# Filling products on TensorE, and new costs and ranks for the planner of a fused attention and two-layer kernel

## The chip, the cores and the metric

One core of a Trainium2 chip runs the whole program. The metric is the device time of one execution in microseconds (us). The profiled execution is a single one; the time of the kernel is the median of several.

## The reference

```python
def _attn_ref(q, k, v):                       # q, k, v: (4, 8, 576, 64)
    scores = scale * np.matmul(q, k.transpose(0, 1, 3, 2))
    mask_plain = (rel >= 0) & (rel < 32)
    mask_dil = (rel >= 0) & (rel < 128) & (rel % 4 == 0)
    ...                                        # plain for heads 0-3, dilated for heads 4-7
    scores = np.where(masks[None], scores, -1e9)
    attn = np.exp(scores - max); attn = attn / (sum + 1e-9)
    return np.matmul(attn, v)

def reference(**kwargs):
    x = attn_out.transpose(0, 2, 1, 3).reshape(2304, 512)
    x = _moe_ref(x, w_in, w_out)      # h = x @ w_in; (h - tanh(h)) @ w_out
    return _moe2_ref(x, w_in, w_out)  # h = x @ w_in; (h * sigmoid(h)) @ w_out
```

The weights are 512 x 2048 and 2048 x 512 for each layer, and arrive as 64-bit numbers.

## The kernel before

Attention is done for a batch at a time, in four pairs of heads; pairs 0 and 1 are plain, 2 and 3 dilated. A pair has nine query blocks of 64 rows, worked in three units of three blocks. In the first batch a unit is: mask and score products into a bank y0 or y1 (`products`, L425 and L432), the maxima on VectorE (L456), the exps with their sums on ScalarE (L469), a reciprocal and the normalisation on VectorE or GpSimd (L474 to L479), the transposition of P on TensorE (L501), its copy to pT on ScalarE (L127 by `p_copy`), the product with v (`values`, L510), and a split of the result into two parts, `x_hi` on ScalarE and `x_lo` on VectorE (L529). Ahead of a pair, q and k are transposed on TensorE (L387 for dilated pairs, L396 for plain ones). In later batches VectorE transposes instead (L416, L492).

Each layer has 16 steps f. A first product `h` takes four chunks c of the 512 features with three passes each (`passes`, L541); a gate (ScalarE and VectorE) gives g, split into two parts; a second product `y` adds into four banks y0 to y3. The first block of 512 tokens needs x of all four pairs of the first batch; the second batch is worked while that block runs.

The weights come in 32 chunks per layer (16 for `w_in`, 16 for `w_out`). A chunk is loaded into a staging buffer (L144, L146), then scaled in two ScalarE passes (`prelu` L160, `lows` L165), shifted on VectorE (L170), joined on GpSimd (L174), copied as the leading part on ScalarE (L127, w) and subtracted for the trailing part (L183).

The order of everything up to the second product of step 13 of the first block is set by a planner. `play` (L93) holds a list of operations, each with the engines it may run on and a cost in us, the operations it follows, a rank, and for loads a landing time `late`. It repeatedly takes the operation that can begin first, by the planned times; of those that begin within 0.02 us on the same engine it takes the one of the lowest rank; and it emits its instructions at once. Each engine's queue is then worked in this order, whatever the true durations are. Chunk work has the rank `due`, step f of the first block `SLOT0 + SLOT * f`, units of the first batch 12 to 32, and pairs of the second batch `NEXT0 + NEXT * c`. The landing of loads is planned as one running sum over all loads. The planner starts TensorE at 6.3 us.

Before it, `WARM` products of 512 columns run on TensorE while the first loads arrive (L723 to L726). The banks y0 and y1 take the scores of units in turn, y2 and y3 the transposed P (`y_bank`, L746).

The lines which a walk through the plan needs are these.

```python
106                for e, c in o.on.items():
107                    if begins[e] + c <= soon:
109            t, e = min((min(x[0] for x in v), e) for e, v in first.items())
110            t, o = min((x for x in first[e] if x[0] <= t + NEAR), key=lambda x: x[1].rank)
117                landed = max(landed, t + 1.5) + o.late
118                o.end = landed + 0.7
```

Of the kernel before, what the change touches and what calls it, by code (L numbers as in the profile page):

```python
# [8 lines left out]
F32 = mybir.dt.float32  # L9
F32R = mybir.dt.float32r  # L10
BF16 = mybir.dt.bfloat16
# [8 lines left out]
P = 128  # L20
QB = 64
ROWS_P, ROWS_D = 96, 72
KB = 96
UB = 3
# [7 lines left out]
def tile_kernel(  # L32
# [47 lines left out]
    class Op:  # L80
# [8 lines left out]
        def shares(self, e):  # L89

            return self.port and e in "VP"

    def play(ops, free):  # L93


        landed = port = 0.0
        todo = list(ops)
        while todo:
            first = {}
            for o in todo:  # L100
                if any(a.end is None for a in o.after):
                    continue
                ready = max((a.end for a in o.after), default=0.0)
                begins = {e: max(free[e], ready, port if o.shares(e) else 0.0) for e in o.on}
                soon = min(begins[e] + c for e, c in o.on.items()) + SLACK
                for e, c in o.on.items():
                    if begins[e] + c <= soon:
                        first.setdefault(e, []).append((begins[e], o))
            t, e = min((min(x[0] for x in v), e) for e, v in first.items())
            t, o = min((x for x in first[e] if x[0] <= t + NEAR), key=lambda x: x[1].rank)  # L110
            o.fn(ENGINE[e])
            free[e] = t + o.on[e]
            if o.shares(e):
                port = free[e]
            o.end = free[e] + JOIN
            if o.late:
                landed = max(landed, t + 1.5) + o.late
                o.end = landed + 0.7
            todo.remove(o)
# [150 lines left out]
    for n in range(NB):  # L270

        for start in range(0, S, CLS):
            at = start - (QB * n - HALO)
            if 0 < at < KB:
                keep(half[:, n, 0:at], [[0, at]], at - HALO - 1, -1)
    nc.scalar.copy(out=mask[QB:], in_=half)
    mask_dil = [mask[:, UB * u:UB * (u + 1)] for u in range(NU)]
    mask_plain = [mask[:, 0::5]] + [mask[:, NB - 1:]] * (NU - 1)

# [263 lines left out]
    class First:  # L543
# [29 lines left out]
        def second_part(self, f, c, g):  # L573
            w = wout[0, f]
            if c == 0 and f == 0:
                self.y = [ps_y.tile([P, 512], F32, tag=f"y{k}", name=f"y{k}")[:, :self.n] for k in range(NC)]
            if True:
                passes(self.y[c], [w[:, a, c * P:(c + 1) * P] for a in range(2)],
                       [g[:, a] for a in range(2)], f == 0, f == NF - 1)
                if f == NF - 1:  # L580
                    hi, lo = self.parts(c)
                    nc.scalar.activation(out=hi, in_=self.y[c], func=AF.Copy)
                    nc.vector.tensor_tensor(out=lo, in0=self.y[c], in1=hi.bitcast(F32), op=ALU.subtract)
# [64 lines left out]
    ATTN_END = max(max(x) for x in STARTS) + 10  # L648


    MORE_OUT = (28, 29, 30, 31)
    MORE_IN = (14, 16, 18, 20, 22, 24, 26, 28)
    WARM = 14

    SLOT0, SLOT, UNIT0, UNIT = 46.0, 5.2, 12.0, 1.8
    DUE = 13.0
    NEXT0, NEXT = 41.0, 20.0
    SLACK, NEAR, JOIN = 0.3, 0.02, 0.05  # L660

    FEED2 = ((1, 1, 1), (1, 1, 2))
# [29 lines left out]
    with tc.manual_schedule():  # L692
# [11 lines left out]
        def op(on, fn, after=(), rank=0.0, late=0.0, port=False):  # L704
            ops.append(Op(on, fn, after, rank, late, port))
            return ops[-1]
# [29 lines left out]
        for p in first:  # L736
            got[p, 0] = op({"S": 1.1 if p.dil else 0.55}, lambda e, p=p: p.load_q(), rank=p.c, late=0.8)
            got[p, 1] = op({"S": 1.1 if p.dil else 0.55}, lambda e, p=p: p.load_k(), rank=p.c + 0.1, late=0.8)
            v_on = {"P": 0.62} if p.dil else {"S": 0.55}
            got[p, "v"] = [op(v_on, fn, rank=p.c + 0.2, late=0.25 if p.dil else 0.5) for fn in p.v_loads()]  # L740
        ring_h, ring_s, ring_t, ring_o, ring_p = (Ring(2) for _ in range(5))
        ring_v = Ring(UB)
        x_done = {}
        early = {}

        def y_bank(n):  # L746
            return ps_y.tile([P, 512], F32, tag=f"y{n}", name=f"y{n}")

        for i, (p, u) in enumerate(units):
            r = p.rank + UNIT * u  # L750
            if u == 0:
                moves = []
                for which in range(2):
                    for half in range(2):
                        held = {}
                        a = op({"T": 0.8}, lambda e, p=p, w=which, h=half, held=held: held.update(m=p.transpose_pe(w, h)),
                               [got[p, which], *ring_h.take()], r - 2 + which * 0.1)
                        moves.append(op({"V": 0.34, "A": 0.36}, lambda e, p=p, w=which, held=held: p.transposed(e, w, held["m"]),
                                        [a], r - 2 + which * 0.1))
# [2 lines left out]
                in_room[2 * p.c + 1] = moves[2:]  # L762
                free_p = ring_p.take()
                early[p] = []
            a = op({"T": 1.0}, lambda e, p=p, u=u, i=i: p.masked_scores(u, y_bank(i % 2)), [*moves, *ring_s.take(), *free_p], r)
            early[p].append(a)
            b = op({"V": 0.38}, lambda e, p=p, u=u: p.maxima(u), [a], r)
            c = op({"A": 1.35}, lambda e, p=p, u=u: p.exps(u), [b], r)
            ring_s.leave(c)
            d = op({"V": 0.36}, lambda e, p=p, u=u: p.sums(UB * u, UB * (u + 1)), [c], r)  # L770
            d = op({"V": 0.4, "P": 0.65}, lambda e, p=p, u=u: p.normed(e, UB * u, UB * (u + 1)), [d], r, port=True)
            t = op({"T": 0.45}, lambda e, p=p, u=u, i=i: p.p_transpose_pe(u, y_bank(2 + i % 2)), [d, *ring_t.take()], r)
            if u == NU - 1:
                ring_p.leave(t)
            m = op({"A": 0.4}, lambda e, p=p, u=u: p.p_copy(e, u), [t, *ring_v.take()], r)
            ring_t.leave(m)
            a = op({"T": 0.6}, lambda e, p=p, u=u, i=i: p.values(UB * u, UB * (u + 1), *((ps_s, "s") if i % 2 else (ps_o, "o"))),
                   [m, *got[p, "v"], *ring_o.take()], r)
            ring_v.leave(a)
            b = op({"A": 0.4}, lambda e, p=p, u=u: p.x_hi(e, UB * u), [a], r)  # L780
# [228 lines left out]
```

## Time and profile before

| | |
|---|---|
| median of 3 runs | 915.97 us (915.05 to 916.33) |
| the profiled execution | 915.71 us, its span 913.9 us |
| TensorE busy | 896.9 us (98%), 5998 products |
| VectorE busy | 436.0 us (48%) |
| ScalarE busy | 398.0 us (44%) |
| GpSimd busy | 122.6 us (13%) |
| mean granted TensorE clock | 0.986 |

The span is the time from the first to the last instruction of the profiled execution. PE is TensorE, DVE VectorE, ACT ScalarE, POOL GpSimd, SP the queue of SyncE. "Busy" counts the time in which an engine has at least one instruction in work; products overlap in TensorE's pipeline, so the durations of single ones add up to more. The granted clock is given as a share of 2.4 GHz. A releaser behind an arrow is the instruction that ended the idle time before.

### The profile page before, as it was taken

What the parts mean: (1) busy time and instruction counts of PE and PEld (TensorE: products, weight loads), DVE (VectorE), ACT (ScalarE), POOL (GpSimd) and SP (SyncE); (2) the same over time, 40 slices, a digit from 0 to 9 for tenths busy, and PEclk for the clock granted to TensorE, in tenths of its full rate; (3) what the DMA queues carried; (4) which work ended last, traced back from release to release, by engine and by line L of the source; (5) the groups of instructions that cost most, each with busy time, mean ns of one, the idle gap of its engine ahead of it and who ended that gap; (6) DMA issues with size and microseconds to landing.
All of it is one profiled execution on the core that took longest, in us unless ns stands there. A gap on an engine that the chain in (4) does not pass through costs nothing.

```text
span 913.9 us, 15235 instructions
## 1 busy us (share of the span) xinstructions
PE 896.9 (98%) x5998; PEld 782.8 (86%) x5998; DVE 436.0 (48%) x836; ACT 398.0 (44%) x969; POOL 122.6 (13%) x164
## 2 busy tenths in 40 slices
PE   7999999999999999999999999999999999999997
PEld 5677778999999999999999888888888888888896
DVE  2468887446756666433266666422222222222232
ACT  5689875334443334423266666432223222322322
POOL 8333553000010000000022222100000000000000
PEclk9599999999999999999999999999999999999999
DMA  9966335213223322024044564140004000200100
GB/s 232 281 153 167 98 96 117 93 28 82 49 50 58 97 35 69 20 70 147 1 141 139 186 214 139 46 136 3 1 1 139 0 1 1 93 0 1 32 15 24
DMA packets 122375, 74.39 MB, mean 81 GB/s; under 512 B 84896, under 2 KB 110528, under 8 KB 122304
## 3 DMA queue, kind: packets, MB, share of 16 engines
q1 hardware_dynamic: 121472, 72.57, 28.6%
q0 software_dynamic: 832, 0.85, 0.4%
q8 instruction: 47, 0.77, 0.4%
q14 instruction: 24, 0.20, 0.1%
HBM read 59.24 MB, written 14.16 MB: 80 GB/s over the span
## 4 chain that ended last, share of the span: by engine, by line
PE 85%; DVE 5%; ACT 4%; issue 2%; DMA 2%; SPq 2%; DVEq 0%; ACTq 0%
PE h L541 39%; PE y L541 39%; PE s L432 3%; PE o L510 2%; DMA st<-in_moe_w_in_dram 1%; ACT w L127 1%; ACT st L160 1%; DVE g L555 1%; DVE pT L492 1%; SPq L359 1%; PE y L432 1%; PE h L387 1%; ACT gg L969 1%; DVE w L183 1%; DVE st L170 1%
## 5 line engine op out<-in xcount | busy, mean ns | idle before, releaser
L541 PE MATMUL h<-x,w 128*128 128x512 f32 (+4 forms) x2304 | 439.5, 338 | 0.8
L541 PEld LDWEIGHTS h<-x,w 128*128 128x128 f32 x2304 | 365.6, 188 | 45.2 <-DVE g L555 2.5
L541 PE MATMUL y<-gg,w 128*128 128x304 f32 (+3 forms) x1344 | 226.8, 314 | 0.0
L541 PE MATMUL y<-w,gg 128*128 128x512 f32 x864 | 209.8, 390 | 0.4 <-ACT gg L969 0.4
L541 PEld LDWEIGHTS y<-gg,w 128*128 128x128 f32 x1344 | 197.6, 188 | 8.8 <-DVE gg L882 0.7
L541 PEld LDWEIGHTS y<-w,gg 128*128 128x128 f32 x864 | 160.8, 188 | 34.3 <-ACT gg L969 1.2
L969 ACT ACTIVATE gg<-g 128x512 fp32r<-128x512 f32 (+4 forms) x176 | 90.7, 515 | 134.5 <-DVE g L555 74.6
L604 DVE SCALAR_TENSOR_TENSOR g<-g,h 128x512 f32<-128x512 f32 (+1 forms) x80 | 50.7, 633 | 200.6 <-ACT g L603 200.6
L971 DVE TENSOR_TENSOR gg<-g,gg 128x512 fp32r<-128x512 f32 (+4 forms) x176 | 96.9, 550 | 102.4 <-ACT gg L969 99.3
L603 ACT ACTIVATE g<-h 128x512 f32<-128x512 f32 (+1 forms) x80 | 44.4, 555 | 201.9 <-PE h L541 201.7
L174 POOL TENSOR_TENSOR st<-st 128x512 int32<-128x512 int32 x64 | 67.3, 1053 | 211.8 <-ACT st L165 179.2
L554 ACT ACTIVATE g<-h 128x304 f32<-128x304 f32 (+2 forms) x96 | 40.2, 418 | 122.6 <-PE h L541 117.8
L555 DVE TENSOR_TENSOR g<-h,g 128x304 f32<-128x304 f32 (+2 forms) x96 | 44.6, 465 | 82.3 <-ACT g L554 81.9
L183 DVE TENSOR_TENSOR w<-st,w 128x512 fp32r<-128x512 f32 x58 | 53.9, 933 | 24.0 <-ACT w L127 23.8
L160 ACT ACTIVATE st<-st 128x512 f32<-128x512 f32 x64 | 43.0, 671 | 8.9 <-DMA st<-in_moe_w_out_dram 4.5
L492 DVE STREAM_TRANSPOSE pT<-prob 32x288 f32<-32x288 f32 x96 | 44.9, 468 | 1.5
L127 ACT ACTIVATE w<-st 128x512 fp32r<-128x512 f32 x64 | 42.4, 664 | 4.0 <-POOL st L174 3.4
L165 ACT ACTIVATE st<-st 128x512 int32<-128x512 uint32 x64 | 43.3, 677 | 0.0
L469 ACT ACTIVATE prob<-prob,nb 128x96 f32<-128x96 f32 x108 | 38.8, 364 | 0.2 <-DVE nb L456 0.2
L479 POOL TENSOR_TENSOR prob<-prob,sum 128x864 f32<-128x864 f32 (+1 forms) x17 | 20.1, 1182 | 114.7 <-DVE sum L475 114.7
L170 DVE TENSOR_SCALAR st<-st 128x512 uint32<-128x512 uint32 x64 | 28.6, 455 | 6.6 <-ACT st L160 4.9
L510 PEld LDWEIGHTS o<-pT,v 96*64 96x64 f32 x576 | 21.6, 146 | 11.8 <-issue 4.3
(61 smaller groups left out, 421.2 us busy)
## 6 DMA issues: line engine op xcount, KB each, us to landing
st<-in_moe_w_in_dram SPq DMA_DIRECT2D x64, 256.0 KB
st<-in_moe_w_out_dram SPq DMA_DIRECT2D x32, 512.0 KB
x<-y_hi SPq DMA_DIRECT2D x4, 1024.0 KB
x<-y_lo SPq DMA_DIRECT2D x4, 1024.0 KB
qin<-in_q_dram SPq DMA_DIRECT2D x48, 72.0 KB
kin<-in_k_dram SPq DMA_DIRECT2D x48, 72.0 KB
v<-in_v_dram SPq DMA_DIRECT2D x16, 192.0 KB
y_hi<-x SPq DMA_DIRECT2D x3, 608.0 KB
```

Source lines behind the costliest of these rows:

```text
L127: engine.activation(out=out, in_=in_, func=AF.Copy, scale=1.0 if scale is None else scale)
L160: engine.activation(out=high, in_=high, func=AF.Prelu, scale=2.0 ** -112, alpha=2.0 ** 32)
L165: engine.activation(out=low.bitcast(I32), in_=low, func=AF.Copy, scale=2.0 ** -29)
L174: engine.tensor_tensor(out=high, in0=high, in1=self.low.bitcast(I32), op=ALU.add)
L183: engine.tensor_tensor(out=self.flat[:, 1], in0=self.high.bitcast(F32), in1=self.flat[:, 0].bitcast(F32), op=ALU.subtract)
L492: nc.vector.transpose(out=pT[32 * kk:32 * kk + 32, :, j, 32 * i:32 * i + 32], in_=self.p[p0:p0 + 32, :, 32 * kk:32 * kk + 32],)
L541: nc.tensor.matmul(o, stat[a], mov[b], start=first and n == 0, stop=last and n == 2)
L555: nc.vector.tensor_tensor(out=g, in0=h, in1=g, op=ALU.subtract)
L603: nc.scalar.activation(out=g, in_=h, func=AF.Tanh, scale=0.5)
L604: nc.vector.scalar_tensor_tensor(out=g, in0=g, scalar=1.0, in1=h, op0=ALU.add, op1=ALU.mult)
L969: nc.scalar.activation(out=gg[:, 0], in_=g, func=AF.Copy)
L971: nc.vector.tensor_tensor(out=gg[:, 1], in0=g, in1=gg[:, 0].bitcast(F32), op=ALU.subtract)
```

## The change

Filling products: `play` gets a function `idle`. When the operation that it takes next is on TensorE, and TensorE's planned idle time before it is long enough, it first emits products of a 128 x 128 bf16 identity with 224 columns of the mask, whose results nobody reads. Their number is the idle time less `IDLE_GAP`, over `IDLE_US`, rounded down; before 12 us of planned time 0.4 us is added to the idle time. They go to columns 288 to 511 of a bank that is `lent`: first the bank of the warming products, then the bank of the scores emitted last, whose columns 0 to 287 hold these scores. With the first second product of the first block, `lent` is emptied and no more are emitted.

Costs and ranks: the planner's costs of TensorE's small products become smaller. `WARM` goes from 14 to 18. `DUE`, which is subtracted in the rank of chunk work, goes from 13 to 6; `NEXT0` and `NEXT` from 41 and 20 to 60 and 16; the first of `MORE_OUT` from 28 to 27, which is the chunk number up to which one extra staging buffer is used.

```diff
+    def idle(us):
+
+        for n in range(int((us - IDLE_GAP) / IDLE_US) if lent else 0):
+            nc.tensor.matmul(lent[0][:, UB * KB:], one[BF16], spare, start=True, stop=True)
 
     def play(ops, free):
 ...
             t, o = min((x for x in first[e] if x[0] <= t + NEAR), key=lambda x: x[1].rank)
+            if e == "T":
+                idle(t - free[e] + (MORE_IDLE if t < 12.0 else 0.0))
             o.fn(ENGINE[e])
 ...
+    spare = mask[:, 0:3].rearrange("p n k -> p (n k)")[:, :512 - UB * KB]
+    lent = []
 ...
             if c == 0 and f == 0:
+                lent.clear()
                 self.y = [ps_y.tile([P, 512], F32, tag=f"y{k}", name=f"y{k}")[:, :self.n] for k in range(NC)]
 ...
-    MORE_OUT = (28, 29, 30, 31)
+    MORE_OUT = (27, 29, 30, 31)
     MORE_IN = (14, 16, 18, 20, 22, 24, 26, 28)
-    WARM = 14
+    WARM = 18
+
+    IDLE_GAP, IDLE_US = 0.3, 0.11
+    MORE_IDLE = 0.4
 ...
-    DUE = 13.0
-    NEXT0, NEXT = 41.0, 20.0
+    DUE = 6.0
+    NEXT0, NEXT = 60.0, 16.0
 ...
+        lent[:] = [bank]
 ...
         def y_bank(n):
-            return ps_y.tile([P, 512], F32, tag=f"y{n}", name=f"y{n}")
+            bank = ps_y.tile([P, 512], F32, tag=f"y{n}", name=f"y{n}")
+            if n < 2:
+                lent[:] = [bank]
+            return bank
 ...
-                        a = op({"T": 0.8}, lambda ...: held.update(m=p.transpose_pe(w, h)),
+                        a = op({"T": 0.5 if p.dil else 0.58}, lambda ...: held.update(m=p.transpose_pe(w, h)),
 ...
-            a = op({"T": 1.0}, lambda ...: p.masked_scores(u, y_bank(i % 2)), ...)
+            a = op({"T": 0.8}, lambda ...: p.masked_scores(u, y_bank(i % 2)), ...)
 ...
-            t = op({"T": 0.45}, lambda ...: p.p_transpose_pe(u, y_bank(2 + i % 2)), ...)
+            t = op({"T": 0.35}, lambda ...: p.p_transpose_pe(u, y_bank(2 + i % 2)), ...)
 ...
-            a = op({"T": 0.6}, lambda ...: p.values(UB * u, UB * (u + 1), ...), ...)
+            a = op({"T": 0.5}, lambda ...: p.values(UB * u, UB * (u + 1), ...), ...)
```

## Rows read from the trace of the kernel before

Times are us from the span's start unless the row says ns. A row of an engine's order of time has its start, its length (overlapping the next by the pipeline), and in brackets the idle time before it; a row of the chain has a start and the time until the next step.

**Rows 1.** The profile's page: busy us and share; granted clock in 40 slices.

```profile
PE 896.9 (98%) x5998; PEld 782.8 (86%) x5998; DVE 436.0 (48%) x836; ACT 398.0 (44%) x969; POOL 122.6 (13%) x164
...
PEclk9599999999999999999999999999999999999999
```

**Rows 2.** Busy time by stretch: stretch, its length, busy of each engine, clock, DMA.

```profile
20.00:25.00 5.00, 1.11 (x30) 0.84 (x27) 2.00 (x7) 3.26 (x16) 4.07 (x7) 0.98 1.08 332
25.00:48.00 23.00, 22.36 (x237) 17.04 (x237) 10.63 (x30) 14.91 (x51) 8.18 (x11) 0.50 1.00 283
48.00:60.00 12.00, 11.06 (x125) 8.24 (x122) 8.17 (x21) 10.16 (x33) 4.85 (x8) 0.97 0.39 94
60.00:110.00 50.00, 50.00 (x349) 38.00 (x348) 43.35 (x85) 46.44 (x116) 19.42 (x21) 1.00 0.57 143
110.00:160.00 50.00, 49.82 (x308) 39.55 (x307) 40.43 (x73) 32.48 (x74) 23.47 (x24) 1.00 0.47 107
160.00:913.00 753.00, 745.84 (x4736) 668.01 (x4734) 325.19 (x605) 280.28 (x654) 46.34 (x53) 1.00 0.22 64
```

**Rows 3.** The same for TensorE by single microseconds: busy, clock, DMA.

```profile
25.00:26.00 1.00, 0.99 (x7) 0.50 1.08 305
...
48.00:49.00 1.00, 1.00 (x17) 0.66 0.16 49
```

**Rows 4.** TensorE in order of time: products with idle time before them.

```profile
24.10 0.57 PE L510 MATMUL o<-pT,v 96*64 96x64 f32 x12 [3.56 <-ACT pT L127]
...
28.29 0.88 PE L501 MATMUL y<-one,prob 128*96 128x128 f32 x3 [0.62 <-POOL prob L479]
...
58.82 0.78 PE L432 MATMUL s<-kT,qT 64*64 64x32 f32 x16 [0.94 <-DVE x L529]
```

**Rows 5.** ScalarE in order of time: the first weight scaling.

```profile
21.74 0.65 ACT L160 ACTIVATE st<-st 128x512 f32<-128x512 f32 x1 [3.75 <-DMA st<-in_moe_w_in_dram]
```

**Rows 6.** The chain that ended last, in order of time.

```profile
22.39 0.97 ACT prob L469 x6
...
31.83 0.84 PE o L510 x12
...
36.54 1.16 PE y L432 x12
37.70 0.81 PE y L501 x3
...
50.25 0.64 PE y L432 x12
50.89 0.50 PE o L510 x12
51.39 0.46 PE y L501 x3
...
64.27 0.68 PE y L541 x3
```

**Rows 7.** ScalarE's groups, 20 to 59 us: count, busy us, mean ns, idle before.

```profile
L469 ACT ACTIVATE prob<-y,nb 128x96 f32<-128x96 f32 x27 | 8.8, 334 | 1.8 <-DVE nb L456 1.8
...
L127 ACT ACTIVATE pT<-y 96x384 f32<-96x384 f32 x10 | 4.9, 488 | 4.7 <-PE y L501 4.7
L127 ACT ACTIVATE x<-o 128x192 fp32r<-128x192 f32 x11 | 4.5, 407 | 2.2 <-PE o L510 2.0
L165 ACT ACTIVATE st<-st 128x512 int32<-128x512 uint32 x6 | 4.0, 670 | 0.0
```

**Rows 8.** TensorE in order of time: the warming products.

```profile
1.47 4.57 PE L725 MATMUL y<-warm 128*128 128x512 bf16 x14 [1.47 <-DVE warm L721]
```

**Rows 9.** ScalarE in order of time: the last chunk's leading copy.

```profile
153.84 0.67 ACT L127 ACTIVATE w<-st 128x512 fp32r<-128x512 f32 x1 [0.51 <-DVE w L183]
```

**Rows 10.** GpSimd in order of time: last value loads, first normalisation.

```profile
26.29 1.25 POOL L359 DMA_DIRECT2D v<-in_v_dram  x2 [0.67 <-DMA v<-in_v_dram]
27.55 0.68 POOL L479 TENSOR_TENSOR prob<-prob,sum 128x288 f32<-128x288 f32 x1
```

More of the change, by code (lines that the diff above doesn't have):

```diff
@@ L755, in tile_kernel @@
                         held = {}
-                        a = op({"T": 0.8}, lambda e, p=p, w=which, h=half, held=held: held.update(m=p.transpose_pe(w, h)),
+                        a = op({"T": 0.5 if p.dil else 0.58}, lambda e, p=p, w=which, h=half, held=held: held.update(m=p.transpose_pe(w, h)),
                                [got[p, which], *ring_h.take()], r - 2 + which * 0.1)
@@ L764, in tile_kernel @@
                 early[p] = []
-            a = op({"T": 1.0}, lambda e, p=p, u=u, i=i: p.masked_scores(u, y_bank(i % 2)), [*moves, *ring_s.take(), *free_p], r)
+            a = op({"T": 0.8}, lambda e, p=p, u=u, i=i: p.masked_scores(u, y_bank(i % 2)), [*moves, *ring_s.take(), *free_p], r)
             early[p].append(a)
@@ L771, in tile_kernel @@
             d = op({"V": 0.4, "P": 0.65}, lambda e, p=p, u=u: p.normed(e, UB * u, UB * (u + 1)), [d], r, port=True)
-            t = op({"T": 0.45}, lambda e, p=p, u=u, i=i: p.p_transpose_pe(u, y_bank(2 + i % 2)), [d, *ring_t.take()], r)
+            t = op({"T": 0.35}, lambda e, p=p, u=u, i=i: p.p_transpose_pe(u, y_bank(2 + i % 2)), [d, *ring_t.take()], r)
             if u == NU - 1:
@@ L776, in tile_kernel @@
             ring_t.leave(m)
-            a = op({"T": 0.6}, lambda e, p=p, u=u, i=i: p.values(UB * u, UB * (u + 1), *((ps_s, "s") if i % 2 else (ps_o, "o"))),
+            a = op({"T": 0.5}, lambda e, p=p, u=u, i=i: p.values(UB * u, UB * (u + 1), *((ps_s, "s") if i % 2 else (ps_o, "o"))),
                    [m, *got[p, "v"], *ring_o.take()], r)
```

## The prediction

> **What bounds the kernel now.** I read four views in this order: the page's busy line and clock line, busy time by stretch, TensorE's instructions in order of time, and the chain that ended last. The page says that TensorE is busy for 98% of the span and that its clock is full in every slice but one [rows 1]. So the end is set by TensorE, and what a change can give back is time in which TensorE is idle or slow. The stretches say where that is: nearly all of it lies in the first 60 us [rows 2]. From 60 to 160 us TensorE is busy for 99.8 of 100 us at full clock, and from 160 us on for 745.8 of 753. The reader should see two losses in the early stretches. Between 20 and 25 us TensorE works for 1.1 of 5 us. From 25 to 48 us it is busy for 22.4 of 23 us, but the granted clock is 0.50, that is 1.2 GHz. By single microseconds the clock falls after that hole and comes back in the 49th [rows 3].
>
> The hole has a cause that can be followed. TensorE waits 3.56 us before a values group (L510) for ScalarE's copy of pT [rows 4]. ScalarE is late because its in-order queue stands 3.75 us at the first scaling of a weight chunk (L160, prelu of chunk 0), whose DMA has not landed before 21.7 us [rows 5]. The planner put that prelu ahead of the exps of the fourth and fifth unit, which follow it as the chain's six exps at 22.39 us [rows 6]; it believed in an earlier landing. So the stall is a misfit of plan and DMA, and its consequence is the long stretch at half clock.
>
> **What the losses are worth.** The chain gives the same groups at both clocks [rows 6]: scores 1.16 and 0.64 us, P transposes 0.81 and 0.46, values 0.84 and 0.50. The ratios are 0.55, 0.57 and 0.60. TensorE's 22.4 us between 25 and 48 us would be 22.4 x 0.55 to 0.60 = 12.3 to 13.4 us at full clock, so 9.0 to 10.1 us are lost to the clock. Idle time ahead of products adds 3.56 + 0.62 + 0.94 = 5.1 us [rows 4]. The ceiling is thus 10.1 + 5.1 = 15.2 us.
>
> **The change part by part.** *Costs and ranks.* Per unit of three query blocks the plan charged TensorE 1.0 + 0.45 + 0.6 and a third of four moves of 0.8, in all 3.1 us, or 37 us for 12 units; now it is 0.8 + 0.35 + 0.5 and four moves of 0.54 over three, 2.4 us or 28 us. Measured at full clock, P transposes and values are 0.46 and 0.50 and scores 0.64 without their mask product [rows 6], so the new numbers are nearer. I walked through the planner's rule by hand with the new costs. Chunk 0's planned landing doesn't move: SyncE's plan reaches it at 11.5 us, and the running landing time is then 2.0 + 8 x 0.8 for q and k + 8 x 0.5 for v + 9 x 0.25 for GpSimd's loads + 1.5 = 16.15, with 0.7 on top 16.9. The scores of the fourth and fifth unit are planned at 13.7 and 15.8 us, their exps at 16.3 and 18.4; with the copies behind them ScalarE is free at 20.6 with no attention work ready, and only there takes the prelu: behind the exps of the fifth unit instead of ahead of the fourth's. That puts two units of ScalarE work ahead of it, 2 x 0.97 us of exps [rows 6] and four copies of about 0.4 each [rows 7], 3.6 us, close to the 3.75 us for which it stood [rows 5]. I take the stall as gone; if chunk 0 lands later, up to the old 3.75 us stay.
>
> *Four more warming products.* Fourteen take 4.57 us [rows 8], 0.33 each, while later products of 512 columns run at 0.68 for three, 0.23 each [rows 6]; so four cost between 0.9 and 1.3 us. In the kernel before, such a delay would vanish under the wait for chunk 0. With that cover gone it counts; I take 0.9.
>
> *Filling products.* Each is a 128x128 bf16 product of 224 columns, so by the 0.23 us of a 512-column product about 0.10 us at full clock and 0.20 at half; the plan counts 0.11. The planner emits them only for planned idle time less 0.3 us, so in a plan that fits they cost nothing. Where TensorE is later than planned, they stand in its in-order queue ahead of real work. By hand the plan is packed on TensorE up to about 20.6 us, so next to none are emitted there; they come later, where ScalarE and the values of the last pair hold TensorE up. That is where the clock was low. They remove no work of another engine, so the new bound is ScalarE.
>
> *What is late next.* From 20 to 59 us ScalarE does 27 exps with their sums, nine units at 0.97 [rows 6], 8.7 us; 4.9 go on pT copies and 4.5 on x copies [rows 7]: 18.1 us of attention work. Starting at 21.7 us that ends at 39.8 at the earliest. Between it the plan must place three chunks or so, each three ScalarE passes of 0.67 us [rows 7]: 6 us more, 45.8. With the warming delay of 0.9 dense work begins at 46.7 instead of 58.8 us [rows 4]: 12.1 us earlier.
>
> *What is given back.* Chunk work is now due 6 instead of 13 us ahead of its slot, and the second batch's attention is ranked 19 us later for its first pair and 7 for its last. Fewer chunks are then ready when dense work starts. ScalarE is busy 46.4 of 50 us and VectorE 43.4 of 50 between 60 and 110 us [rows 2]. Two chunks' worth more on ScalarE is 2 x 2.0 = 4 us, and 46.4 + 4 exceeds 50 by 0.4; if it cannot spread beyond 110 us, where ScalarE has 17.5 us free, TensorE waits 0.4 to 4 us. I take 2. The last chunk's leading copy starts only at 153.84 us [rows 9], a few microseconds ahead of the end of this stage, so the supply has little slack at its end too. MORE_OUT moves one staging buffer by one chunk; no row shows a price. I bound it by one chunk's three ScalarE passes, 2.0 us either way [rows 7], and take 0, as only one of the last chunks is moved.
>
> *A wait that the fillers may add.* They write columns 288 to 511 of the score bank filled last, while VectorE and ScalarE read columns 0 to 287 of it. No trace here shows such a case. The price of one wait lies between 0 and one unit's exps, 0.97 us [rows 6]; over the few gaps in which those exps have started but not ended I take 1.5 us in all.
>
> The Trainium skill's page "PSUM — Partial Sum Buffer", section "PSUM bank collisions raise a hardware error", says that two engines at one bank and quadrant collide even at disjoint columns and that such accesses must be guarded by bank. By that rule every filler has to be ordered behind the reads of that bank and each later read behind the fillers; without it the 1.5 us would be 0. No run here shows it yet.
>
> **Sum.** 915.7 (the profiled run) - 12.1 + 2 + 1.5 = 907.1 us; the profiled run lies 0.3 us under the median of 915.97, within the spread of the three. I predict **907 us**, with its own range from 901 (nearly the whole ceiling, nothing given back) to 911 (four more us given back, by the bounds above).
>
> **The rivals.** *The clock falls again.* GpSimd issues the value loads of the dilated pairs until 27.55 us and only then takes a normalisation [rows 10]; TensorE already waited 0.62 us on one [rows 4]. If attention gets there earlier by the 3.75 us of the old stall, that wait grows by as much, in place of the one removed, and a hole of that size was followed by half clock before. Fillers then run at 0.20 us and delay real work, though they may also bring the clock back sooner. If half of the 12.1 us is kept, and half of the give-back of 3.5 with it, 915.7 - 6 + 1.75 = 911; 908 to 914.
> *The gain is given back later.* TensorE starts early, but chunks and second-batch attention, limited by ScalarE, VectorE and the staging loads, come at their old times, and TensorE idles between 60 and 160 us instead. For it speak 46.4 and 43.4 of 50 us; against it, that after 110 us ScalarE is only 65% busy [rows 2]. Then 914, from 912 to 916.
> *It fills nothing where it matters.* The plan sees no idle time in the 3.56 us hole, because the wait is one for a DMA that it holds landed; if the order doesn't move either, the clock falls as before: 915, 914 to 917.
> *Slower.* Every gap makes TensorE wait for the exps of the bank filled last, and the fillers run after that wait instead of during it: 0.97 + about 0.5 us of fillers per gap. What is left of the gain, 12.1 - 2 = 10.1 us, is eaten at seven such gaps, and 12 of them, one for each unit, make 12 x 1.5 = 18 us: 915.7 - 10 + 18 = 924. It decides from the eighth gap on. The page named above describes why such waits would be needed.
>
> **How the numbers follow.** Forecast 0.52, clock falls again 0.20, given back later 0.10, fills nothing 0.08, slower 0.10. A difference of 0.2%, 1.8 us, is about what a measurement of this kernel tells from none. Faster by more: 0.52 + 0.19 + 0.05 + 0.02 = 0.78. Within it: 0.01 + 0.04 + 0.05 = 0.10. Slower: 0.10 + 0.01 + 0.01 = 0.12. The range reaches from 901 to 915: it leaves out the slower case, parts of the two cases near 915, and a few in a hundred below.
>
> **What would show it.** Right: the granted clock stays at 1.00 from 20 to 60 us; ScalarE stands less than 1 us at the first L160; filling products appear after 20 us, and the second batch's first scores, now at 58.82, start near 47; TensorE is still near 50 of 50 us in the stretches behind. Wrong: a slice at 0.50 in the first 60 us (clock falls again), holes in TensorE with waits for chunks or pT between 50 and 150 us (given back), waits of the filling products for ScalarE's exps of about 1 us each (slower), or less than ten fillers (fills nothing). A first second product later than 60 us, now at 64.3 [rows 6], would refute the main term.

## The result, and the profile after

| | kernel before | kernel after |
|---|---|---|
| median (runs) | 916.15 us (915.05 to 917.30, 4) | 908.50 us (906.94 to 909.53, 4) |
| the profiled execution: time, span | 915.7 us, 913.9 us | 909.49 us, 907.7 us |
| granted clock, mean | 0.986 | 0.997 |
| instructions of TensorE | 5998 | 6028 |
| ratio, 95% interval | | 0.9915 (0.9893 to 0.9937) |

The change takes 7.7 us off, 0.85%. The prediction was 907, from 901 to 915, so the time lies inside; the steps behind it held less well than the number. Executions of one kernel differ in where the granted clock falls, so a trace shows one case, and the medians decide.

The profile's page of the kernel after, the same two lines as [rows 1]:

```profile
PE 892.7 (98%) x6028; PEld 779.9 (86%) x6028; DVE 434.3 (48%) x834; ACT 397.0 (44%) x967; POOL 130.2 (14%) x168
...
PEclk9999999999999999999999999999999999999999
```

6028 - 5998 = 30 more products: four warming ones and only 26 filling ones, all of them behind 35 us, so the 0.4 us that is added before 12 us of planned time brought none. The clock line has a 9 in every slice now.

Busy time by stretch, kernel after, columns as in [rows 2]:

```profile
20.00:25.00 5.00, 4.97 (x108) 4.01 (x106) 4.05 (x12) 3.77 (x17) 3.89 (x7) 1.00 1.09 335
25.00:48.00 23.00, 20.51 (x316) 16.29 (x313) 13.12 (x40) 16.80 (x67) 9.95 (x17) 0.93 0.95 256
110.00:160.00 50.00, 48.65 (x314) 39.39 (x313) 36.45 (x68) 31.81 (x70) 19.17 (x20) 1.00 0.41 115
```

Between 20 and 25 us TensorE works for 4.97 us instead of 1.11, and from 25 to 48 us the clock is 0.93 instead of 0.50. In that stretch it is idle for 2.5 us, 1.59 of them in one wait (below). From 110 to 160 us it is busy for 48.65 instead of 49.82: that is what is given back. Single microseconds, columns as in [rows 3], show what is left of the half clock (the clock is the first number after the five engines):

```profile
40.00:41.00 1.00, 0.12 (x2) 0.12 (x2) 0.14 (x1) 0.83 (x6) 0.24 (x1) 1.00 0.94 174
41.00:42.00 1.00, 1.00 (x10) 0.90 (x9) 0.21 (x2) 0.00 (x0) 0.61 (x1) 0.75 0.81 113
42.00:43.00 1.00, 1.00 (x7) 0.88 (x6) 0.00 (x0) 0.00 (x0) 0.06 (x1) 0.50 0.75 97
44.00:45.00 1.00, 1.00 (x8) 0.82 (x7) 0.65 (x2) 1.00 (x3) 0.00 (x0) 0.55 0.91 141
```

It falls in the 42nd and comes back in the 45th microsecond: some 3.4 us instead of the nearly 24 of [rows 3]. ScalarE in order of time, kernel after, the first weight scaling:

```profile
25.23 0.68 ACT L167 ACTIVATE st<-st 128x512 f32<-128x512 f32 x1
```

No idle time stands before it; the 3.75 us of [rows 5] are gone. It comes at 25.23 us, and the chunk had landed by 21.74 in [rows 5]. TensorE in order of time, kernel after (start, length, idle time before in brackets). L405 are transposes of q and k, L510 P transposes, L519 values, L96 filling products, L441 scores, L550 products of the chunks:

```profile
1.47 6.95 PE L738 MATMUL y<-warm 128*128 128x512 bf16 x18 [1.47 <-DVE warm L734]
...
12.14 0.72 PE L405 MATMUL h<-one,qin 96*64 96x96 f32 x12 [1.07 <-ACT kT L134]
...
38.76 0.53 PE L510 MATMUL y<-one,prob 128*96 128x128 f32 x3
40.88 1.66 PE L96 MATMUL y<-mask,one 128*128 128x224 bf16 x11 [1.59 <-ACT prob L478]
42.34 0.85 PE L510 MATMUL y<-one,prob 128*96 128x128 f32 x3
42.98 2.35 PE L96 MATMUL y<-mask,one 128*128 128x224 bf16 x13
45.59 0.92 PE L519 MATMUL o<-pT,v 96*64 96x64 f32 x24
47.83 4.41 PE L550 MATMUL h<-x,w 128*128 128x512 f32 x18
52.37 0.78 PE L441 MATMUL s<-kT,qT 64*64 64x32 f32 x16
53.88 1.54 PE L550 MATMUL y<-gg,w 128*128 128x512 f32 x6
...
148.21 0.57 PE L519 MATMUL o<-pT,v 96*64 96x64 f32 x12 [1.21 <-DVE x L538]
...
191.29 0.78 PE L441 MATMUL s<-kT,qT 64*64 64x32 f32 x16
```

What to see in these rows. There is no hole of 3.56 us before a values group [rows 4] any more. The filling products stand in two groups, of eleven and of thirteen, and the first waits 1.59 us for ScalarE's exps: the bank that they write still has to be read. The clock falls at about 41.5 us, 0.6 us after that wait, so the thirteen take 2.35 us. Unbroken work on the chunks begins at 47.83 us; in the kernel before, it began with the scores at 58.82 [rows 4]. The first second product comes at 53.88 instead of 64.11 (64.27 in the chain of [rows 6]). At 148.21 a values group waits 1.21 us for VectorE's part of the split into x (`x_lo`, L538); TensorE had no such wait before.

**How far the gain goes.** The last row, the first scores of the second batch in the next block, is a mark that all kernels here share. In the trace of before it is this row:

```profile
197.68 0.78 PE L432 MATMUL s<-kT,qT 64*64 64x32 f32 x16
```

In that of after it is at 191.29, 6.39 us earlier. The spans differ by 913.9 - 907.7 = 6.2. From the mark to the end both take 716.2 to 716.4 us. So all of it is decided ahead of 191 us.

### The profile page after: what moved, and what is told of

The parts are those of the page before. It is cut to its first block, busy times and chain, and to the rows that moved or that the text cites. A ratio compares the mean times of both kernels' runs of the same rounds, so it can differ in the third digit from the quotient of the medians.

```text
span 907.7 us, 15318 instructions
## 1 busy us (share of the span) xinstructions
PE 892.7 (98%) x6028; PEld 779.9 (86%) x6028; DVE 434.3 (48%) x834; ACT 397.0 (44%) x967; POOL 130.2 (14%) x168
## 3 DMA queue, kind: packets, MB, share of 16 engines
q1 hardware_dynamic: 121472, 72.57, 28.8%
## 4 chain that ended last, share of the span: by engine, by line
PE 87%; DVE 6%; ACT 4%; issue 2%; DMA 1%; POOL 0%; DVEq 0%; POOLq 0%; ACTq 0%
PE h L550 40%; PE y L550 39%; PE s L441 3%; PE o L519 2%; ACT w L134 1%; DVE pT L501 1%; DVE g L564 1%; ACT st L167 1%; PE y L738 1%; DVE w L190 1%; ACT gg L986 1%; PE y L441 1%; PE y L510 1%; DVE x L593 1%; DMA st<-in_moe_w_out_dram 1%
## 5 line engine op out<-in xcount | busy, mean ns | idle before, releaser
L550 PE MATMUL h<-x,w 128*128 128x512 f32 (+4 forms) x2304 | 439.5, 338 | 0.9
L550 PEld LDWEIGHTS h<-x,w 128*128 128x128 f32 x2304 | 365.7, 188 | 45.6 <-DVE g L564 3.1
L550 PE MATMUL y<-gg,w 128*128 128x304 f32 (+3 forms) x1344 | 226.2, 313 | 0.0
L550 PE MATMUL y<-w,gg 128*128 128x512 f32 x864 | 209.8, 390 | 0.4 <-ACT gg L986 0.4
L550 PEld LDWEIGHTS y<-gg,w 128*128 128x128 f32 x1344 | 197.9, 188 | 8.8 <-ACT w L134 0.4
L550 PEld LDWEIGHTS y<-w,gg 128*128 128x128 f32 x864 | 160.8, 188 | 34.3 <-ACT gg L986 1.2
L181 POOL TENSOR_TENSOR st<-st 128x512 int32<-128x512 int32 x64 | 69.5, 1091 | 206.9 <-ACT st L172 167.9
L190 DVE TENSOR_TENSOR w<-st,w 128x512 fp32r<-128x512 f32 x53 | 50.8, 962 | 26.1 <-ACT w L134 26.1
L501 DVE STREAM_TRANSPOSE pT<-prob 32x288 f32<-32x288 f32 x96 | 44.9, 468 | 1.4
L488 POOL TENSOR_TENSOR prob<-prob,sum 128x864 f32<-128x864 f32 (+1 forms) x15 | 17.8, 1184 | 106.6 <-DVE sum L484 105.9
L441 PE MATMUL s<-kT,qT 64*64 64x96 f32 (+1 forms) x480 | 26.5, 245 | 2.3 <-DVE kT L425 2.0
```

Of the source, the lines that this page charges most:

```text
L181: engine.tensor_tensor(out=high, in0=high, in1=self.low.bitcast(I32), op=ALU.add)
L190: engine.tensor_tensor(out=self.flat[:, 1], in0=self.high.bitcast(F32), in1=self.flat[:, 0].bitcast(F32), op=ALU.subtract)
L441: nc.tensor.matmul(s[QB * j:QB * (j + 1), m, at:at + size], self.qT[64 * j:64 * j + 64, QB * n:QB * n + QB], self.kT[64 * j:64 * j + 64, k ...
L501: nc.vector.transpose(out=pT[32 * kk:32 * kk + 32, :, j, 32 * i:32 * i + 32], in_=self.p[p0:p0 + 32, :, 32 * kk:32 * kk + 32],)
L550: nc.tensor.matmul(o, stat[a], mov[b], start=first and n == 0, stop=last and n == 2)
```

## The experiments

All kernels are compared with runs of the kernel before on the same chip.

**Which part carries the gain: no filling products.**

```diff
-        for n in range(int((us - IDLE_GAP) / IDLE_US) if lent else 0):
+        for n in range(0):
```

> The changed kernel without its 26 filling products; four more warming products, new costs and ranks stay. In its profile 11 fillers wait 1.59 us for the exps of the last unit and run at 40.88 to 42.34 us, 13 more at 42.98 to 45.17 us, while the P transposes behind them had their input at 40.3 and 42.1 us. Theory order (the gain comes from the new costs, which move chunk 0's prelu; the fillers only delay): about 3 us faster than the changed kernel, 905.5 us. Theory clock (the fillers keep the clock up): the clock falls in the wait for the last P transposes and stays at half speed for several us, 911 to 914 us.

908.37 us (906.69 to 909.22, 4 runs), ratio 0.9916 (0.9903 to 0.9928): the same as with them. TensorE in order of time, and single microseconds with the clock as the first number after the five engines:

```profile
38.51 0.53 PE L510 MATMUL y<-one,prob 128*96 128x128 f32 x3
40.13 0.53 PE L510 MATMUL y<-one,prob 128*96 128x128 f32 x3 [1.09 <-POOL prob L488]
41.86 0.54 PE L510 MATMUL y<-one,prob 128*96 128x128 f32 x3 [1.20 <-POOL prob L488]
42.33 1.53 PE L519 MATMUL o<-pT,v 96*64 96x64 f32 x24
...
52.12 0.78 PE L441 MATMUL s<-kT,qT 64*64 64x32 f32 x16
```

```profile
42.00:43.00 1.00, 1.00 (x16) 0.82 (x17) 0.80 (x2) 0.89 (x2) 0.03 (x1) 0.70 0.80 93
49.00:50.00 1.00, 1.00 (x6) 0.83 (x5) 0.00 (x0) 0.04 (x1) 0.60 (x1) 0.89 1.37 212
```

In the medians the filling products make no difference, and neither theory's time came. The traces show two effects that cancel. From the P transposes at 38.51 to the values at 42.33 are 3.82 us here; with filling products, from 38.76 to 45.59, 6.83. So they delay TensorE by 3.0 us. But without them it waits 1.09 and 1.20 us for GpSimd, the clock falls at 42.4 and stays at 1.2 GHz for 7 us, and from the values to the second batch's first scores are 52.12 - 42.33 = 9.79 us, against 52.37 - 45.59 = 6.78. That costs 3.0 us. The sum is zero. (This execution was at half clock from 11.7 to 15.1 us as well, ahead of these rows.)

**Fourteen warming products in the changed kernel.**

```diff
-    WARM = 18
+    WARM = 14
```

> The changed kernel with 14 instead of 18 warming products. In the profile of the changed kernel they end 2.4 us later than in the kernel before, and all early attention with them. Theory order: that delay reaches the end, since the wait for chunk 0 that used to hide it is gone: 1 to 2.4 us faster, 906 to 907.5 us. Rival (the warming holds the clock through the first attention units): a stretch at 0.50 appears before 30 us and the time is 910 us or more. Rival (still hidden): 908.5 us.

909.45 us (907.27 to 911.28, 6 runs), 0.9929 (0.9917 to 0.9941). No gain from starting earlier. The four products aren't a cost that reaches the end. Whether they help is not settled here: the profiled execution, 910.88 us, has a second stretch at half clock, from 28.8 to 35.6 us, that the one of the changed kernel lacks.

**New costs alone, in the kernel before** (the old ranks, 14 warming products, no filling products).

```diff
-            t = op({"T": 0.45}, ...
+            t = op({"T": 0.35}, ...
...
```

> The kernel before with the new costs of TensorE's small products alone: old ranks, 14 warming products, no fillers. Chunk 0's prelu is planned at 20.59 us instead of 18.78 us. Theory order: no stall of 3.75 us at chunk 0, full clock until 38 us, 905 to 908 us. Theory clock (fillers needed): half clock again, 912 to 916 us. If the ranks carry the gain: 912 us or more with a full clock.

908.85 us (907.97 to 912.22, 6 runs), 0.9929 (0.9917 to 0.9940). The costs alone bring nearly the whole gain, though a little less than the theory of the order asked. TensorE in order of time:

```profile
39.37 0.53 PE L510 MATMUL y<-one,prob 128*96 128x128 f32 x3 [1.09 <-POOL prob L488]
41.09 0.87 PE L510 MATMUL y<-one,prob 128*96 128x128 f32 x3 [1.20 <-POOL prob L488]
```

The hole before the values is gone, as in the kernel after, and the same two waits for GpSimd remain as in the kernel without filling products. In this trace the clock is at half from 40.6 to 47.4 us.

**Filling products and 18 warming ones alone** (old costs and ranks).

```diff
+        for n in range(int((us - IDLE_GAP) / IDLE_US) if lent else 0):
+            nc.tensor.matmul(lent[0][:, UB * KB:], one[BF16], spare, ...)
...
```

> The kernel before with fillers and 18 warming products, old costs and ranks. In this plan TensorE has no idle time before 49 us that gives a filler, and chunk 0's prelu stays ahead of the fourth unit's exps. Theory order: the stall and the stretch at half clock stay, 915.5 to 917.5 us. Theory clock: 908 to 912 us.

916.69 us (915.17 to 918.06, 11 runs), 1.0011 (0.9997 to 1.0025): nothing. TensorE in order of time (L519 and L510 are the values and P transposes):

```profile
24.49 0.57 PE L519 MATMUL o<-pT,v 96*64 96x64 f32 x12 [1.40 <-ACT pT L134]
...
30.06 0.88 PE L510 MATMUL y<-one,prob 128*96 128x128 f32 x3 [2.02 <-POOL prob L488]
...
58.99 1.23 PE L96 MATMUL y<-mask,one 128*128 128x224 bf16 x11
```

The plan emits eleven filling products, at 58.99 us, when the clock has long come back. The real holes, 1.40 us for ScalarE's pT and 2.02 us for GpSimd, are none in the plan, and nothing fills them. The shorter hole of 1.40 us is followed by the half clock too, from 25.2 to 49.1 us.

**New ranks alone** (`DUE`, `NEXT0`, `NEXT`, `MORE_OUT`).

> The kernel before with the new ranks (DUE, NEXT0, NEXT, MORE_OUT) alone. Chunk 0's prelu stays planned at 18.78 us. Theory order by costs: the stall and the half clock stay, 915 to 917 us. Rival (the ranks carry part of the gain): 911 to 913 us.

922.32 us (921.39 to 923.27, 4 runs), 1.0070 (1.0055 to 1.0085): 6 us slower. The hole before the values is 3.67 us here, the clock at half from 22 to 49 us. So the ranks don't remove the stall. On the old plan they cost more than either theory allowed: between 86 and 160 us TensorE has six waits, 4.1 us in all, where the kernel before has one of 0.18. In this order the values that the kernel returns are wrong (relative error 0.10), so something is read or written out of turn, where isn't known; its time only says what such an order takes. On the new plan the kernel after and the kernel with new costs alone lie within each other's intervals.

**Is it the clock? One hole filled by hand** (the kernel before, its order unchanged, with 16 products of 512 columns into a bank that nobody reads at the time, ahead of the values where it waits 3.56 us).

```diff
+            if i == 2:
+                fn = a.fn
+                a.fn = lambda e, fn=fn: (hole(), fn(e))
```

> The kernel before, in its own order, with 16 products of 512 columns placed in the real hole of TensorE (20.5 to 24.1 us), into a bank that nobody reads then; nothing else changes. The hole itself stays. Theory clock (the half clock is what costs, and work in the hole keeps it up): full clock from 25 to 48 us, 907 to 910 us. Rival (the gain of the change is the removed wait of 3.75 us and the order, the half clock costs little because other engines set the pace): 915 to 916 us, whatever the clock does.

916.11 us (908.81 to 917.72, 12 runs), 0.9992 (0.9970 to 1.0014). That median hides two outcomes: ten executions at a mean clock of 0.988 to 0.991 and 915.75 to 917.72 us, and two at 1.000, at 908.81 and 909.16. One of the ten was profiled; TensorE in order of time and the stretch by its busy times (L756 fills, L501 are P transposes):

```profile
21.95 3.63 PE L756 MATMUL y<-mask,one 128*128 128x512 bf16 x15
...
30.19 0.53 PE L501 MATMUL y<-one,prob 128*96 128x128 f32 x3 [2.45 <-POOL prob L479]
```

```profile
25.00:48.00 23.00, 20.55 (x240) 15.20 (x238) 9.94 (x29) 14.30 (x47) 8.77 (x12) 0.63 0.98 272
```

The trace has 15 of the 16 products. The hole at 22 us is filled and the clock kept through it. The next hole, 2.45 us for GpSimd's normalisation, isn't filled, and after it the clock is at half from 31.2 to 51.7 us. In the kernel before this wait was 0.62 us [rows 4]. TensorE was ready for it at the same time, 28.29 - 0.62 = 27.67 us there and 30.19 - 2.45 = 27.74 here; GpSimd was later, not TensorE earlier.

The two outcomes are of one and the same program: 916.4 us, the median of the ten, and 909.0, the mean of the two. So about 20 us at half clock cost 7.4 us.

**Both holes filled** (11 more, ahead of the P transposes that wait for GpSimd).

```diff
+            if i == 4:
+                tfn = t.fn
+                t.fn = lambda e, fn=tfn: (hole(11), fn(e))
```

> The order of the kernel before, with products into a bank nobody reads in both of its real holes: 16 of 512 columns ahead of the third unit's values (DVE's and ScalarE's wait) and 11 ahead of the fifth unit's P transposes (GpSimd's wait, 2.45 us in the kernel with one hole filled). Theory (the gain of the change is the clock): the granted clock stays at 1.00 from 20 to 60 us in most executions, and the time falls to about 909, as in the two executions of the kernel with one hole filled that kept their clock (908.8 and 909.2). Rival (the gain is the idle time that the new plan removes): 915 to 916, since the waits themselves stay as long as they were.

910.42 us (909.85 to 911.15, 6 runs), 0.9941 (0.9919 to 0.9964), all six at a clock of 0.999 or 1.000. The same two views:

```profile
21.98 3.63 PE L756 MATMUL y<-mask,one 128*128 128x512 bf16 x16
...
27.70 2.55 PE L756 MATMUL y<-mask,one 128*128 128x512 bf16 x11
30.48 0.53 PE L501 MATMUL y<-one,prob 128*96 128x128 f32 x3 [0.24 <-POOL prob L479]
...
36.95 0.53 PE L501 MATMUL y<-one,prob 128*96 128x128 f32 x3 [0.92 <-POOL prob L479]
...
53.65 0.78 PE L432 MATMUL s<-kT,qT 64*64 64x32 f32 x16 [0.93 <-DVE x L529]
```

```profile
25.00:48.00 23.00, 21.72 (x315) 15.18 (x313) 15.57 (x42) 18.09 (x69) 10.03 (x16) 1.00 0.96 275
```

With both holes filled the old order gains 916.09 - 910.42 = 5.7 us, and 58.82 - 53.65 = 5.2 us at the second batch's first scores. Neither theory gave the number quite: 909 is within reach, 915 to 916 is out. The clock itself is worth more than that, since here too GpSimd is late: the P transposes of the second hole come at 30.48 us instead of 28.29 [rows 4]. From them to the second batch's first scores the kernel before takes 58.82 - 28.29 = 30.5 us, this one 53.65 - 30.48 = 23.2, which is 7.4 less, a new wait of 0.92 us for GpSimd included. Both holes still take their time, 3.63 and 2.55 us, now busy with products that nobody reads. The kernel before agrees with the theory of the clock by itself: 3 of its 44 executions beside these kernels had a clock of 0.994, and took 909.99 to 910.10 us.

**The filling products in another bank** (that of the scores one unit earlier, which have been read).

```diff
             if n < 2:
-                lent[:] = [bank]
+                lent[:] = last
+                last[:] = [bank]
```

> The changed kernel with its fillers written to the score bank filled one before the last, whose exps are over, instead of the last. In the profile of the changed kernel the first filler of the long group waits 1.59 us for the last unit's exps, the clock falls during that wait, and 24 fillers at 1.2 GHz hold the P transposes up by 3 us. Theory wait (this wait spoils the fillers): they start at once, run at full clock, no stretch at 0.50 near 42 us, first second product 3 us earlier, 905.5 us. Rival (the fillers can't hold the clock, or their wait costs nothing that isn't lost otherwise): 908 to 909 us.

906.22 us (905.72 to 910.34, 6 runs), 0.9901 (0.9885 to 0.9917). TensorE in order of time:

```profile
38.29 0.53 PE L510 MATMUL y<-one,prob 128*96 128x128 f32 x3
38.66 1.22 PE L96 MATMUL y<-mask,one 128*128 128x224 bf16 x11
...
40.04 1.41 PE L96 MATMUL y<-mask,one 128*128 128x224 bf16 x13
41.65 0.53 PE L510 MATMUL y<-one,prob 128*96 128x128 f32 x3 [0.20 <-POOL prob L488]
42.11 0.92 PE L519 MATMUL o<-pT,v 96*64 96x64 f32 x24
...
44.35 4.41 PE L550 MATMUL h<-x,w 128*128 128x512 f32 x18
48.88 0.78 PE L441 MATMUL s<-kT,qT 64*64 64x32 f32 x16
...
187.73 0.78 PE L441 MATMUL s<-kT,qT 64*64 64x32 f32 x16
```

The same eleven and thirteen products, with no wait ahead of them and at full clock: 1.22 and 1.41 us instead of 1.66 and 2.35. From the P transposes to the values are 42.11 - 38.29 = 3.82 us, just what the kernel without filling products needs. They lie wholly in the waits for GpSimd now, of which 0.20 us is left. Chunk work begins at 44.35, and the mark of the next block comes at 187.73, 3.56 us ahead of the changed kernel's. That is one trace against one trace. The medians don't settle it: the ratio is 0.9901 here and 0.9915 and 0.9912 in the two groups of the changed kernel, and their intervals overlap.

The Trainium skill's page "PSUM — Partial Sum Buffer", section "PSUM bank collisions raise a hardware error", wants accesses of two engines to one bank ordered even where their columns differ. The two traces agree: 1.59 us of waiting for the exps in the bank just filled, none in the bank before it.

**That, and a later planned landing of GpSimd's value loads.**

```diff
-                o.end = landed + 0.7
+                o.end = t + 13.0 if o.late == 0.25 else landed + 0.7
```

> The kernel with fillers in the other bank, and with the planned landing of GpSimd's value loads put at 13 us after their start in the plan instead of behind all loads planned before them. The values of the last pair are then planned 2.8 us earlier, ahead of the last P transposes. Theory (planned landing is what holds the last pair up): 904 to 906 us. Rival (the last pair is held by the chain of exps, normalisation and P transposes, not by its loads): same as the kernel with fillers in the other bank within 0.5 us.

911.73 us (911.24 to 914.38, 6 runs), 0.9956 (0.9944 to 0.9969): 5.5 us worse than without it, at a clock of 0.999 in the profiled execution. The first second product comes at 51.16 us, near the 50.39 without it; but between 78 and 143 us TensorE has six waits of 0.18 to 1.28 us, 4.3 in all, for weights, kT, gg and pT, and reaches the mark of the next block at 193.23 instead of 187.73. The theory that a truer landing time must help falls, and so does the rival that nothing changes: the gain was given back, in part. In this order too the returned values are wrong (relative error 0.13), for a reason that isn't known.

**That other bank with 14 warming products, and the changed kernel once more beside it.**

> The changed kernel with its fillers in the other bank, and 14 instead of 18 warming products. If the later end of the warming (about 1.2 to 2.4 us in the profiled executions) reaches the end of the kernel: about 905, a ratio near 0.988. Rival (it is hidden, as ScalarE and the loads set the time that follows, or the clock falls early as it did in the changed kernel with 14): 906 to 909.

> The changed kernel unaltered, on the same chip and beside the same runs of the kernel before as the others of this group: 908 to 909, a ratio of 0.991 to 0.993. If the other bank is worth something, its kernels lie 1 to 3 us below it.

906.91 us (905.96 to 907.61, 5 runs), 0.9904 (0.9881 to 0.9927), and 907.45 us (906.55 to 909.24, 5 runs), 0.9912 (0.9889 to 0.9936), the ratio as expected and the time a little below. Four warming products more or less change nothing that can be told, and against the changed kernel the other bank shows 0.5 us here, which is inside the spread. The profiled execution of the changed kernel, 909.24 us, lost its clock at another place; its busy times by stretch, and TensorE in order of time:

```profile
10.00:12.00 2.00, 1.38 (x19) 0.91 (x20) 0.00 (x0) 1.60 (x3) 2.00 (x4) 0.78 1.13 209
20.00:21.00 1.00, 1.00 (x13) 0.82 (x12) 0.00 (x0) 1.00 (x6) 1.00 (x3) 0.50 1.00 268
```

```profile
10.62 0.82 PE L405 MATMUL h<-one,qin 96*64 96x96 f32 x12 [1.08 <-ACT kT L134]
...
42.38 1.21 PE L96 MATMUL y<-mask,one 128*128 128x224 bf16 x11 [1.59 <-ACT prob L478]
...
45.42 0.92 PE L519 MATMUL o<-pT,v 96*64 96x64 f32 x24
```

Here the clock falls at about 11 us; in the 21st microsecond it is still 0.50, and after the 22nd it is full. TensorE waits 1.08 us ahead of it for ScalarE's copy of kT; the other trace of the same kernel has 1.07 us at that place, and the clock stays. The wait of the filling products is 1.59 us in both, and here the clock stays at 1.00 through it. That splits the 3.0 us by which they delayed TensorE in the other trace: from the first filling product to the values are 45.59 - 40.88 = 4.71 us there and 45.42 - 42.38 = 3.04 here, so 1.7 us are the half clock and 1.3 the wait.

**A third hole filled by hand** (the kernel with the other bank, and six more products ahead of the sixth unit's P transposes, which wait for GpSimd).

```diff
+            if i == 5:
+                tfn = t.fn
+                t.fn = lambda e, fn=tfn: (hole(), fn(e))
```

> The changed kernel with its fillers in the other bank, and six more products of 224 columns, into a bank nobody reads, ahead of the sixth unit's P transposes, where TensorE waits for GpSimd. Theory (what is left to gain before 60 us is the clock that falls in some executions): 905.5 to 906.5, with no execution above 908. Rival (the clock is already kept, and the spread to 910 comes from elsewhere): 906 to 907 with the spread of the kernel without these six.

906.10 us (905.53 to 906.21, 5 runs), 0.9894 (0.9872 to 0.9917), every execution at a clock of 1.000. Against the changed kernel on the same chip, 907.45 (906.55 to 909.24), the ranges don't meet: all runs of this version lie below all runs of either kernel beside it. TensorE in order of time (L772 are the six):

```profile
30.51 0.75 PE L772 MATMUL y<-mask,one 128*128 128x224 bf16 x6
...
49.36 0.78 PE L441 MATMUL s<-kT,qT 64*64 64x32 f32 x16
```

The six cover the wait that stood there (0.42 us in the trace without them), and the second batch's first scores come at 49.36, not earlier than the 48.88 without. The median is that of the kernel without these six too; what is new is that no execution lies above 906.21, where the other reached 910.34. That one had 6 runs, on another chip, so the smaller spread is likely the clock but not proved.

## Why the prediction was right, and where it wasn't

**The cause of the loss: right.** ScalarE's stall at chunk 0's prelu made the hole, and the hole the half clock. The new costs alone put the prelu behind two more units and remove it, as the walk through the plan said; the filling products alone and the ranks alone leave it. One reading was loose: the six pieces at 22.39 us in the chain are the exps of one unit, three with the reads of their three sums; the other unit's follow at 23.94.

**What the clock is worth: somewhat too high.** The ratio of equal groups gave 9.0 to 10.1 us for 22.4 us of work, 0.40 to 0.45 for each microsecond at half clock. With both holes filled, 20.4 us at half clock behind the P transposes at 28.29 were worth 7.4 us, 0.36 each; most of the rest went into a wait of 0.92 us for GpSimd that the faster TensorE runs into. The half clock ahead of 28.29 cost nothing in the kernel before, as its work ended in a wait for GpSimd anyway; so the ceiling of 15.2 us counted some us twice, as clock and as waiting. The net gain of 5.2 to 5.7 is smaller still because GpSimd took its normalisation about 2 us later in these traces. A full clock isn't needed for that: with the filling products alone, at half clock, it was nearly as late (P transposes at 30.06, after 2.02 us of waiting).

**The main term, -12.1: the step that failed.** It had two errors. Dense work began at 47.83 instead of 46.7 us, because the filling products held TensorE up by 3.0 us; in the kernel with the other bank it began at 44.35, so the sum of ScalarE's work, 18.1 + 6, was no bound. ScalarE is busy for 16.80 of 23 us from 25 to 48, and by 47.8 us it has done six of the nine chunk passes that I had charged. Second, I set the start of unbroken work against the scores at 58.82 and didn't ask what lay ahead of each. Ahead of 58.82 the kernel before had done 18 chunk products, ahead of 47.83 the kernel after three; at 0.23 us each [rows 6] the 15 that are missing are 3.4 us. So the term should have read 58.82 - 47.83 - 3.4 = 7.6.

**Given back, +2: right in kind, not in place.** It is 1.2 us, the wait for VectorE at 148.21. The traces with the new costs and the new ranks have it, the one with the new costs and the old ranks doesn't (it has five smaller waits between 60 and 160 us, 1.4 in all). The reason that I gave was another, chunks that come late because ScalarE is full between 60 and 110 us; there ScalarE is busy for 46.6 of 50 us as before, and TensorE for 49.9. 7.6 - 1.2 = 6.4 is the 6.39 us measured at the mark. The other bank gives the same sum: 58.82 - 44.35 - 3.4 - 1.2 = 9.9, and 197.68 - 187.73 = 9.95.

**The filling products' wait, +1.5: one wait, where I thought of several.** It took 1.59 us, more than the upper bound of 0.97 for one, because the exps began at 39.77 us, when TensorE had been done with its P transposes for half a microsecond (38.76 + 0.53 = 39.29). The bound assumed that they had begun. With the products behind it at half clock the price was 3.0 us, against the kernel without filling products, and the half clock there was 3.4 us long instead of 7, which gave as much back. That they stand "where the clock was low" was wrong: 24 of the 26 stand behind 40 us, and the hole that mattered was never idle time in the plan.

**The warming, +0.9: not seen at the end.** Eighteen took 6.95 us in the profiled execution, 2.4 more than fourteen had [rows 8]; with 14 in place of 18 the time is the same (906.91 and 906.22 us with the other bank).

**The sum.** 915.7 - 12.1 + 2 + 1.5 came near the 909.5 of the profiled execution, 2.4 us off, since the main term, 4.5 us too large, was partly offset by two others: 0.8 us too much given back, and 1.5 us for a wait that the measured start of dense work already holds. So the nearness of the number is luck; the mechanism and its sign were earned.

**The checks that were named.** ScalarE stands 0 us at the first scaling, as said; filling products appear after 20 us; the first second product is at 53.88, well ahead of 60. The second batch's scores at 52.37 instead of 47 were the sign of the faulty term. The clock isn't at 1.00 from 20 to 60: 3.4 us are missing.

**The rivals.** "The clock falls again" was right that a half clock follows waits for GpSimd, as the kernels without filling products show, but for 7 us. The wait that it named, behind the value loads, grew from 0.62 to only 0.83 us (31.68 in the trace of after), and the clock held through it; the waits that mattered stand about 9 us later. "The gain is given back later" took 1.2 us. "It fills nothing where it matters" is true of the filling products in their own right and false of the change, whose costs did move the order. "Slower" had its mechanism right, 1.59 us and products behind it, at one place instead of eight.

**What stays open.** Why the clock falls after a wait of about 1.1 us in one execution and is kept after 1.59 in another. Why GpSimd issues its last value loads until 27.55 us in the trace of the kernel before and until 29.1 to 29.7 in those of the kernel after, of the filling products alone, and of one and of both holes filled. What the ranks are worth on top of the new costs.

## What to carry to other kernels

A product that only keeps TensorE busy is worth something where TensorE really waits, not where a plan believes it idle, so read the holes out of a trace; and give it a bank that no engine still has to read. When two starts of "dense work" are compared, count the work that lies ahead of each, or take a mark that both kernels reach with the same work done, as the scores of the next block here. And a stretch at half clock is not quite worth its work times the ratio: subtract the waits that the faster engine will run into, and leave out the part that ended in a wait anyway.

## What the runs showed of the hardware

- The same kernel, with the same waits to 0.01 us, lost its clock at about 11 us in one execution (back in the 22nd microsecond) and at about 41.5 in another (back in the 45th). What TensorE did before was alike but for the start: the warming products took 5.42 us in the first and 6.95 in the second.
- A microsecond at 1.2 GHz cost less than the ratio of equal groups says, 0.40 to 0.45 us: 0.36 between the P transposes at 28.29 us and the second batch's scores (7.4 us for 20.4), as much between two outcomes of one program (7.4 for about 20), and 0.3 for the early fall: from the row that waits for kT to the first filling product of the long group are 42.38 - 10.62 = 31.8 us with half clock from about 11 to 21, and 40.88 - 12.14 = 28.7 without. The slower TensorE no longer waits 0.27 and 0.83 us there.
- Twenty-four filling products in one place, some of them at half clock, were followed by full clock after 3.4 us, where the real work alone needed 7. That they were the reason isn't shown: the kernel without them had a stretch of the same length, from 11.7 to 15.1 us, on real work alone. Twelve runs with one of two holes filled kept the clock twice, six with both filled kept it always.
- Waits of nearly the same length were followed by half clock in one execution and not in another: 1.08 us and 1.07 us for kT, 1.59 us in both for the exps.
